# Top-32 attention with a highway layer: one list of 72 maxima in place of 144, folds over two pairs at once

## The chip, the cores and the metric

One core of a Trainium2 chip runs the whole program. The metric is the device time of one execution in microseconds (us); lower is better. Before the change three runs gave 965.99, 966.19 and 967.7 us, median 966.19.

## The reference

```python
# q, k, v: (8 batches, 8 heads, 576 rows, 64), fp32
scores = scale * np.matmul(q, k.transpose(0, 1, 3, 2))          # 576 x 576 for each batch and head
kth = np.partition(scores, -32, axis=-1)[..., -32:-31]          # 32nd largest score of each row
scores = np.where(scores >= kth, scores, -1e9)
attn = softmax(scores);  x = attn @ v                           # back to 4608 x 512
H = np.maximum(x @ w_h, 0.0);  T = sigmoid(x @ w_t + b_t)
out = T * H + (1.0 - T) * x
```

## The kernel before, in words

A *tile* is 128 query rows of one head against all 576 keys. Two tiles make a *pair*; the program numbers 144 pairs, 18 to a batch. Four pairs (two at the end of a batch, where the last 64 rows of two heads share a tile) make a *group*, 40 in all, and a finished group goes through the highway layer.

The instructions are pinned: each engine runs its own in the order in which they are written, so `keep_in_program_order` (L35) is the line that the profile gives for nearly all of them, and tiles are told apart by name. The main loop (L636) is a software pipeline. In step n:

- VectorE (DVE) folds pair n (`tree`, L181): `hi`, the larger of score i and score i+288, read from the scores in PSUM (`ps`) and their copy in SBUF (`z`); then `hh`, the larger of the two halves of `hi`, 144 wide.
- GpSimd (POOL) forms the smaller ones that the folds threw away (`minima`, L194): `hl` (144 wide) and `lo` (288 wide), by integer subtraction and addition, two instructions each.
- DVE runs the lists of pair n-1 (`chain`, L207), the two tiles in turns: MAX8 and MATCH_REPLACE8 on `hh` twice (the best 16 out of 144), MAX8 on the two halves of `hl` and on `lo` (8 each), all gathered in `w2` (168 wide); then `m3`, a replace, and `m4`, whose last entry is the 32nd largest score.
- ScalarE (ACT) makes the penalties `pen` of pair n-2 from `m4` (`mask`), TensorE (PE) transposes `z` plus penalty (`trans`), ACT takes the exponential (`et`), PE multiplies pair n-3 with v (`av`).
- PE computes the scores of pair n+1 into `ps`, which has one buffer: it waits for `hi` of pair n. ACT copies them to `z` (`evac`), and `hi` of pair n+1 waits for that.
- At a group's end DVE forms `rinv`, POOL normalises `x`, and over the next three steps PE transposes x (`xtps`, in a PE queue where later scores stand behind it), the two matrix products follow, DVE forms `d` twice, POOL adds `o`, and a DMA stores it. `settle` puts margins in `room`, `slack` and `reach` on POOL. If a margin is ever violated, an exact second pass runs.

Of the kernel before, what the change touches and what calls it, by code (L numbers as in the profile page):

```python
# [9 lines left out]
ALU = mybir.AluOpType  # L10
AX = mybir.AxisListType
FP32 = mybir.dt.float32
# [5 lines left out]
TINY = 1.0e-20  # L18
WIDE = 600.0
J = 4  # L20
NZ = 6
NPEN = 3


class Pinned:


    def __init__(self, tc, engine):
        self._tc, self._engine = tc, engine
# [33 lines left out]
class Ops:  # L63


    def __init__(self, ctx, tc, shared, exact):
        self.nc = tc.nc if exact else PinnedCore(tc)
        self.__dict__.update(shared)
        self.exact = exact
        s = "g" if exact else ""  # L70

        def pool(name, bufs, **kw):
            return ctx.enter_context(tc.tile_pool(name=name + s, bufs=bufs, **kw))

# [76 lines left out]
    def scores(self, n, g, pi, prep):  # L153
# [13 lines left out]
                    )  # L167
        self.st[n] = dict(ps=ps)

    def evac(self, n):  # L170
        nc, P, S = self.nc, self.P, self.S
        ps = self.st[n]["ps"]
        if self.exact:
            sc = self.scpool.tile([P, 2, S], FP32, tag="sc", name="sc")
            nc.scalar.copy(sc[:], ps[:, :, 0:S])
        else:
            sc = self.zbufs[n % NZ][:, :, 0:S]
            nc.scalar.activation(sc, ps[:, :, 0:S], AF.Relu)
        self.st[n]["sc"] = sc

    def tree(self, n):  # L181
        nc, P, S = self.nc, self.P, self.S
        H1, H2 = S // 2, S // 4
        sc = self.st[n]["sc"]
        hi = self.treepool.tile([P, 2, H1], FP32, tag="hi", name="hi")
        lo = self.treepool.tile([P, 2, H1], FP32, tag="lo", name="lo")
        hh = self.treepool.tile([P, 2, H2], FP32, tag="hh", name="hh")
        hl = self.treepool.tile([P, 2, H2], FP32, tag="hl", name="hl")
        ps = self.st[n].pop("ps")
        nc.vector.tensor_tensor(hi[:], ps[:, :, 0:H1], sc[:, :, H1:S], ALU.max)  # L190
        nc.vector.tensor_tensor(hh[:], hi[:, :, 0:H2], hi[:, :, H2:H1], ALU.max)
        self.st[n]["tree"] = (hi, hh, hl, lo)

    def minima(self, n):  # L194


        H1, H2 = self.S // 2, self.S // 4
        gp, S = self.nc.gpsimd, self.S
        hi, hh, hl, lo = self.st[n]["tree"]
        sci, hii, loi = [a.bitcast(I32) for a in (self.st[n]["sc"], hi[:], lo[:])]  # L200
        hhi, hli = hh[:].bitcast(I32), hl[:].bitcast(I32)
        gp.tensor_tensor(hli, hii[:, :, 0:H2], hhi, ALU.subtract)
        gp.tensor_tensor(hli, hli, hii[:, :, H2:H1], ALU.add)
        gp.tensor_tensor(loi, sci[:, :, 0:H1], hii, ALU.subtract)
        gp.tensor_tensor(loi, loi, sci[:, :, H1:S], ALU.add)

    def chain(self, g, t, hh, hl, lo):  # L207


        nc, P, S = self.nc, self.P, self.S  # L210
        H2, H4 = S // 4, S // 8
        W = H2 + 24
        vec = nc.vector
        m1, m2, m4 = g.m1[:, t, :], g.m2[:, t, :], g.m4[:, t, :]
        w2 = g.w2[:, t, :]
        vec.max(m1, hh)
        yield
        w1 = self.wpool.tile([P, H2], FP32, tag="w1", name="w1")
        vec.match_replace(w1[:], m1, hh, NEG)
        yield  # L220
        vec.max(m2, w1[:])
        yield
        vec.match_replace(w2[:, 0:H2], m2, w1[:], NEG)
        yield
        vec.max(w2[:, H2 : H2 + 8], hl[:, 0:H4])
        yield
        vec.max(w2[:, H2 + 8 : H2 + 16], hl[:, H4:H2])
        yield
        vec.max(w2[:, H2 + 16 : W], lo)
        yield  # L230
        m3 = self.wpool.tile([P, 8], FP32, tag="m3", name="m3")
        vec.max(m3[:], w2)
        yield
        w3 = self.wpool.tile([P, W], FP32, tag="w3", name="w3")
        vec.match_replace(w3[:], m3[:], w2, NEG)
        yield
        vec.max(m4, w3[:])

    def chain_exact(self, g, t, cur):
        nc, P, S = self.nc, self.P, self.S  # L240
# [15 lines left out]
                yield  # L256

    def lists(self, n, g, pi):
        nc, P, S, H = self.nc, self.P, self.S, self.H
        if pi == 0:  # L260
            for name in ("m1", "m4") if self.exact else ("m1", "m2", "m4"):
                setattr(g, name, self.lpool.tile([P, H, 8], FP32, tag=name, name=name))
            if not self.exact:
                g.w2 = self.lpool.tile([P, H, S // 4 + 24], FP32, tag="w2", name="w2")
        t0 = 2 * pi
        if self.exact:
            sc = self.st[n]["sc"]
            gens = [self.chain_exact(g, t0 + i, sc[:, i, :]) for i in range(2)]
        else:
            hi, hh, hl, lo = self.st[n].pop("tree")  # L270
            gens = [
                self.chain(g, t0 + i, hh[:, i, :], hl[:, i, :], lo[:, i, :])
                for i in range(2)
            ]
        return gens
# [25 lines left out]
    def mask(self, n, g, pi, tis=(0, 1)):  # L301
        nc, P, S = self.nc, self.P, self.S
        sc = self.st[n]["sc"]
        z = self.zbufs[n % NZ]
        pen = None if self.exact else self.pens[n % NPEN]
        for ti in tis:
            t = 2 * pi + ti
            if self.exact:
                low = self.wpool.tile([P, S], FP32, tag="wk", name="low")
                nc.vector.tensor_scalar(  # L310
                    low[:], sc[:, ti, :], g.m4[:, t, 7:8], NEG, ALU.is_lt, ALU.mult
                )
                nc.vector.scalar_tensor_tensor(
                    out=z[:, ti, 0:S],
                    in0=sc[:, ti, :],
                    scalar=g.m1[:, t, 0:1],
                    in1=low[:],
                    op0=ALU.subtract,
                    op1=ALU.add,
                )  # L320
            else:
                nc.scalar.activation(
                    pen[:, ti, 0:S],
                    sc[:, ti, :],
                    AF.Relu,
                    bias=g.m4[:, t, 7:8],
                    scale=-1.0,
                )
        self.st[n].update(z=z, pen=pen)
# [158 lines left out]
def kernel(  # L488
# [31 lines left out]
    nc.vector.tensor_scalar_mul(nident[:], ident[:], -STEEP)  # L520
    zbufs = []
    for i in range(NZ):
        zt = const([P, 2, nck * P], FP32, f"z{i}")
        nc.gpsimd.memset(zt[:, :, S : nck * P], NEG)
        zbufs.append(zt)
    pens = []
# [28 lines left out]
    with ExitStack() as cm:  # L555
# [77 lines left out]
        early[0][4]()  # L633
        ffn = []
        step = 0
        while step < NPR + 4 or ffn:  # L636
            n = step
            if n + 1 < NHP:
                for piece in early[n + 1][1:4]:
# [4 lines left out]
                load_weights()  # L644
            if have(n):
                ops.tree(n)
                ops.minima(n)
            if weights and n > 2:
                cast_weights()
            if have(n - 2):  # L650
                ops.mask(n - 2, *pairs[n - 2], tis=(0,))
            post = None
            if ffn:
                pre, post = ffn.pop(0)
                pre()
            if have(n - 3):
                g, pi = pairs[n - 3]
                ops.av(n - 3, g, pi, preps[g.b][2])
            if have(n - 2):
                ops.mask(n - 2, *pairs[n - 2], tis=(1,))  # L660
            if have(n + 1):
                g, pi = pairs[n + 1]
                ops.scores(n + 1, g, pi, preps[g.b])
                ops.evac(n + 1)
            if n + 1 < NHP:
                early[n + 1][4]()
            gens = ops.lists(n - 1, *pairs[n - 1]) if have(n - 1) else []
            ops.run(gens, 4)
            if post:
                post()  # L670
            ended = have(n - 3) and pairs[n - 3][1] == len(pairs[n - 3][0].pairs) - 1
            if ended:
                ops.run(gens, 5)
                ops.norm(pairs[n - 3][0])
            ops.run(gens)
            if have(n - 2):
                ops.trans(n - 2)
            for piece in pieces.pop(n, []):
                piece()
            if have(n - 1):  # L680
                g, pi = pairs[n - 1]
                if pi == len(g.pairs) - 1:
                    ops.settle(g)
            if ended:
                g = pairs[n - 3][0]
                ffn += [
                    (lambda g=g: ops.ffn_x(g), None),
                    (lambda g=g: ops.ffn_h(g), lambda g=g: ops.ffn_d(g)),
# [90 lines left out]
```

## Time and profile before

| | |
|---|---|
| median of three runs | 966.19 us |
| the profiled execution, its span | 965.6 us, 963.7 us |
| DVE busy | 906.9 us (94% of the span) |
| POOL, PE, ACT busy | 763.5, 749.1, 710.6 us |
| mean granted TensorE clock | 0.902 of full speed |

A row of the timeline gives the start, the busy time and the operation; busy times of neighbours on DVE overlap by a little under 0.1 us, so the cost of an instruction in a full queue is the distance from its start to the next one's start.

### The profile page before, as it was taken

The page shows a single profiled execution, that of the slowest core. Times are in us where ns is not written, and L with a number is a line of the kernel's source. Part 1 is how long each engine was busy: PE and PEld are TensorE (multiplying, and loading weights), DVE is VectorE, ACT ScalarE, POOL GpSimd, SP SyncE. Part 2 cuts the span into 40 slices and gives each one's busy share as a digit, 9 for nine tenths or more (in the row PEclk, how much of TensorE's full clock was granted, in tenths as well). Part 3 has the DMA queues.
Part 4 walks back from the last instruction along what each step waited for, and adds up shares of the span by engine and source line. Part 5 has one row for each costly group of instructions (what it writes and reads, how often), then busy time and mean ns, then how long its engine had stood idle before and what let it go on. Part 6 is the DMA issues. An engine that isn't in the chain of part 4 may idle for free.

```text
span 963.7 us, 20478 instructions
## 1 busy us (share of the span) xinstructions
PE 749.1 (78%) x6554; PEld 524.6 (54%) x6601; DVE 906.9 (94%) x4162; ACT 710.6 (74%) x1321; POOL 763.5 (79%) x802
## 2 busy tenths in 40 slices
PE   5757887878887887778877878787887788777874
PEld 3545555655655555556555555555555555545552
DVE  2879999999999999999999999999999999999992
ACT  3748777887777877787776877688777787767762
POOL 6798888788878878888887788878887787888861
PEclk8779998999898999899998999899999899989896
DMA  5622110122101320022101212012200110000000
GB/s 115 180 64 49 48 49 13 43 50 69 29 12 43 72 63 12 17 71 64 49 12 40 53 49 50 12 44 56 67 25 12 44 49 12 12 18 12 13 12 20
DMA packets 123332, 41.52 MB, mean 43 GB/s; under 512 B 117457, under 2 KB 117457, under 8 KB 123217
## 3 DMA queue, kind: packets, MB, share of 16 engines
q1 hardware_dynamic: 122000, 39.84, 16.5%
q8 instruction: 54, 0.88, 0.4%
q14 instruction: 62, 0.50, 0.2%
q10 hardware_dynamic: 1216, 0.30, 0.1%
HBM read 30.67 MB, written 9.44 MB: 42 GB/s over the span
## 4 chain that ended last, share of the span: by engine, by line
DVE 79%; POOL 8%; PE 7%; SPq 2%; ACT 1%; issue 1%; DMA 1%; POOLq 0%; DVEq 0%
DVE w L35 37%; DVE m L35 22%; DVE hi L35 9%; DVE hh L35 6%; DVE d L35 5%; POOL lo L35 3%; PE ps L35 3%; POOL hl L35 2%; PE zt L35 1%; PE xtps L35 1%; POOL x L35 1%; SPq L103 1%; PE zr L35 1%; SPq L100 1%; ACT z L35 1%
## 5 line engine op out<-in xcount | busy, mean ns | idle before, releaser
L35 PE MATMUL ps<-kT,qT 64*128 64x64 f32 (+3 forms) x1280 | 232.4, 491 | 68.3 <-DVE hi L35 67.9
L35 ACT ACTIVATE pen<-z,m 128x576 bf16<-128x576 f32 x288 | 224.4, 780 | 66.0 <-DVE m L35 65.9
L35 DVE MAX8 m<-w 128x8 f32<-128x168 f32 (+1 forms) x864 | 235.6, 318 | 0.0
L35 PE MATMUL zt<-ident,z 128*128 128x128 f32 x1152 | 234.5, 296 | 0.0
L35 PE MATMUL zt<-nident,pen 128*128 128x128 bf16 x1152 | 222.6, 230 | 0.0
L35 POOL TENSOR_TENSOR hl<-hi,hh 128x288 int32<-128x288 int32 x144 | 114.5, 795 | 125.8 <-DVE hh L35 125.8
L35 ACT ACTIVATE z<-ps 128x1152 f32<-128x1152 f32 x144 | 163.1, 1132 | 67.9 <-PE ps L35 65.1
L35 POOL TENSOR_TENSOR lo<-lo,z 128x576 int32<-128x576 int32 x144 | 203.7, 1414 | 11.3
L35 PEld LDWEIGHTS ps<-kT,qT 64*128 64x128 f32 (+1 forms) x1280 | 116.6, 198 | 174.2 <-issue 94.5
L35 POOL TENSOR_TENSOR lo<-z,hi 128x576 int32<-128x576 int32 x144 | 203.4, 1412 | 0.0
L35 PEld LDWEIGHTS zt<-ident,z 128*128 128x128 f32 x1152 | 175.3, 152 | 22.4
L35 ACT ACTIVATE et<-zt 128x512 bf16<-128x512 f32 x288 | 166.9, 600 | 26.0 <-PE zt L35 25.0
L35 DVE MATCH_REPLACE8 w<-m,w 128x144 f32<-128x144 f32 (+1 forms) x576 | 173.5, 313 | 0.0
L35 PEld LDWEIGHTS <-pen 128*128 128x128 bf16 x1440 | 165.3, 115 | 1.8 <-ACT pen L35 1.7
L35 DVE TENSOR_TENSOR hi<-ps,z 128x576 f32<-128x576 f32 x144 | 108.3, 752 | 28.7 <-ACT z L35 28.6
L35 POOL TENSOR_TENSOR hl<-hl,hi 128x288 int32<-128x288 int32 x144 | 114.7, 797 | 11.3
L35 DVE MAX8 w<-lo 128x8 f32<-128x288 f32 x288 | 116.6, 450 | 0.3 <-POOL lo L35 0.3
L35 PEld LDWEIGHTS <-et 128*128 128x128 bf16 (+1 forms) x1600 | 71.7, 104 | 38.1 <-ACT et L35 14.8
L35 DVE MAX8 w<-hl 128x8 f32<-128x72 f32 x576 | 91.5, 226 | 0.0
L35 PE MATMUL zr<-v,et 128*128 128x65 bf16 (+1 forms) x1600 | 85.1, 199 | 6.0 <-ACT et L35 4.1
L35 PE MATMUL xtps<-ident,x 128*128 128x128 f32 (+1 forms) x160 | 29.6, 316 | 74.8 <-POOL x L35 73.3
L35 PE MATMUL zr<-ident,z 128*128 128x128 f32 x288 | 80.1, 331 | 4.8 <-ACT xs L35 4.8
(62 smaller groups left out, 1103.8 us busy)
## 6 DMA issues: line engine op xcount, KB each, us to landing
kin<-in_k_dram SPq DMA_DIRECT2D x64, 128.0 KB, 2.6
vin<-in_v_dram SPq DMA_DIRECT2D x64, 128.0 KB, 2.6
out_dram<-o SPq DMA_DIRECT2D x32, 256.0 KB, 2.2
qin<-in_q_dram SPq DMA_DIRECT2D x62, 128.0 KB, 2.6
kin<-in_k_dram SPq DMA_DIRECT2D x64, 16.0 KB, 2.3
vin<-in_v_dram SPq DMA_DIRECT2D x64, 16.0 KB, 2.3
w<-in_moe_w_h_dram SPq DMA_DIRECT2D x2, 512.0 KB, 4.2
w<-in_moe_w_t_dram SPq DMA_DIRECT2D x2, 512.0 KB, 7.4
```

Of the source, the lines that this page charges most:

```text
L35: return self._tc.keep_in_program_order(fn(*args, **kw))
L100: eng.dma_start(t[:, 0:J, hh, :], src(h, 0, JP).rearrange("(p j) d -> p j d", j=J))
L103: eng.dma_start(t[0:R, J, hh, :], src(h, JP, S))
```

## The change

- Folds from `hh` on run once for two pairs (a *quad*, 4 tiles): `tree` only forms `hi`; in odd steps `folds` forms `hh` (4 x 144), a third level `h3` (4 x 72) and, straight into `w2`, the 72 smaller values of that level.
- The lists start on `h3`: 72 wide in place of 144. `w2` stays 168 wide: what is left of `h3`, the 72 smaller ones, and 24 from `hl` and `lo`.
- `minima` runs once for a quad and overwrites `hh` and `hi` with `hl` and `lo`; a dependency that was added by hand lets it start after the folds.
- The chain is cut in two: `tops` (four tiles in turns) in the even step after the folds, `rest` two tiles in the next odd step and two late ones reaching into the even step behind it. Masks, transposes, `av` and the highway layer come two steps later.
- `z` has three buffers of four tiles in place of six of two.

```diff
-NZ = 6
+NZ = 3
 def tree(self, n):
+        if n % 2 == 0:
+            self.quads[k] = tuple(
+                self.treepool.tile([P, 4, w], FP32, tag=name, name=name, bufs=bufs)
+                for name, w, bufs in (("hi", H1, 3), ("hh", H2, 3), ("h3", H3, 2))
+            )
-        nc.vector.tensor_tensor(hi[:], ps[:, :, 0:H1], sc[:, :, H1:S], ALU.max)
-        nc.vector.tensor_tensor(hh[:], hi[:, :, 0:H2], hi[:, :, H2:H1], ALU.max)
+        nc.vector.tensor_tensor(
+            hi[:, half, :], ps[:, :, 0:H1], self.st[n]["sc"][:, :, H1:S], ALU.max
+        )
+    def folds(self, k, g, pi):
+        vec.tensor_tensor(hh[:], hi[:, :, 0:H2], hi[:, :, H2:H1], ALU.max)
+        a, b = hh[:, :, 0:H3], hh[:, :, H3:H2]
+        vec.tensor_tensor(h3[:], a, b, ALU.max)
+        return vec.tensor_tensor(
+            g.w2[:, 2 * pi : 2 * pi + 4, H3:H2], a, b, ALU.min
+        )
 def minima(self, k, after):
-        gp.tensor_tensor(hli, hii[:, :, 0:H2], hhi, ALU.subtract)
-        gp.tensor_tensor(hli, hli, hii[:, :, H2:H1], ALU.add)
-        gp.tensor_tensor(loi, sci[:, :, 0:H1], hii, ALU.subtract)
-        gp.tensor_tensor(loi, loi, sci[:, :, H1:S], ALU.add)
+        head = gp.tensor_tensor(hhi, hii[:, :, 0:H2], hhi, ALU.subtract)
+        self.tc.add_manual_dep(
+            head.ins,
+            after.ins.name,
...
+        )
+        gp.tensor_tensor(hhi, hhi, hii[:, :, H2:H1], ALU.add)
+        gp.tensor_tensor(hii, sci[:, :, 0:H1], hii, ALU.subtract)
+        gp.tensor_tensor(hii, hii, sci[:, :, H1:S], ALU.add)
-    def chain(self, g, t, hh, hl, lo):
+    def tops(self, g, t, h3, hl):
-        vec.max(m1, hh)
+        vec.max(m1, h3)
...
+    def rest(self, g, t, lo):
         vec.max(w2[:, H2 + 16 : W], lo)
...
 main loop
-            if have(n - 2):
-                ops.mask(n - 2, *pairs[n - 2], tis=(0,))
+            if have(n - 4):
+                ops.mask(n - 4, *pairs[n - 4], tis=(0,))
...
-            gens = ops.lists(n - 1, *pairs[n - 1]) if have(n - 1) else []
-            ops.run(gens, 4)
-            if post:
-                post()
...
+            if n % 2:
+                gens = ops.lists_rest(n // 2 - 1, *pairs[n - 3]) if have(n - 3) else []
+                late = gens[2:]
+                gens = gens[0:2]
+                ops.run(gens)
+                if post:
+                    post()
+                ops.run(late, 2)
+            else:
+                ops.run(late)
+                gens = ops.lists(n - 2, *pairs[n - 2]) if have(n - 2) else []
+                ops.run(gens, 2)
+                if post:
+                    post()
+                if ended:
+                    ops.norm(pairs[n - 5][0])
+                ops.run(gens)
```

On DVE, a step of the steady part before (`w` with a number is `w1`, `w2` or `w3`, `m` is `m1` to `m4`; sizes are those of the output):

```order
L35 TENSOR_TENSOR hi<-ps,z_69 128x576
L35 TENSOR_TENSOR hh<-hi 128x288
L35 MAX m_8820<-hh 128x8 x2
L35 MATCH_REPLACE w_8918<-m_8820,hh 128x144
L35 MATCH_REPLACE w_8920<-m_8820,hh 128x144
L35 MAX m_8821<-w_8918 128x8
L35 MAX m_8821<-w_8920 128x8
L35 MATCH_REPLACE w_8823<-m_8821,w_8918 128x144
L35 MATCH_REPLACE w_8823<-m_8821,w_8920 128x144
L35 MAX w_8823<-hl 128x8 x4
L35 MAX w_8823<-lo 128x8 x2
L35 MAX m_8932<-w_8823 128x8
```

The whole list of one pair stands behind the folds of the next pair. Now an odd step on DVE, from its `hi` to the `hi` of the even step (`h` is `h3`; `hi` as the input of a MAX is what was `lo`):

```order
L35 TENSOR_TENSOR hi<-ps,z_69 128x576
L35 TENSOR_TENSOR hh<-hi 128x576
L35 TENSOR_TENSOR h_8600<-hh 128x288
L35 TENSOR_TENSOR w_8691<-hh 128x4x72
L35 MAX w_8313<-hi 128x8 x2
L35 MAX m_8730<-w_8313 128x8
L35 MAX m_8732<-w_8313 128x8
L35 MATCH_REPLACE w_8734<-m_8730,w_8313 128x168
L35 MATCH_REPLACE w_8736<-m_8732,w_8313 128x168
L35 MAX m_8437<-w_8734 128x8
L35 MAX m_8437<-w_8736 128x8
L35 MAX w_8313<-hi 128x8 x2
```

The three folds now stand in a row behind the second `hi` of a quad, and the list work between them and the next `hi` belongs to the quad before.

On POOL, before, around the end of a group (a store's `o` and a normalised `x` next to each other, as at one place in a batch):

```order
L35 TENSOR_TENSOR hl<-hi,hh 128x288
L35 TENSOR_TENSOR hl<-hl,hi 128x288
L35 TENSOR_TENSOR lo<-z_65,hi 128x576
L35 TENSOR_TENSOR lo<-lo,z_65 128x576
L35 TENSOR_TENSOR o<-x,d 64x512
L35 TENSOR_TENSOR x<-xs,rinv 128x512
```

Two short ones follow the four of one pair. And now, the two kinds of quad that take turns (one with `room`, one with `o` and `x`):

```order
L35 TENSOR_TENSOR hi<-z_67,hi 128x1152
L35 TENSOR_TENSOR hi<-hi,z_67 128x1152
L35 TENSOR_TENSOR room<-m_9414,w_9284 128x24
L35 TENSOR_TENSOR slack<-m_9413,m_9414 128x8
L35 COPY reach<-m_9412 128x8
L35 TENSOR_TENSOR hh<-hi,hh 128x576
L35 TENSOR_TENSOR hh<-hh,hi 128x576
L35 TENSOR_TENSOR hi<-z_69,hi 128x1152
L35 TENSOR_TENSOR hi<-hi,z_69 128x1152
L35 TENSOR_TENSOR o<-x,d 128x512
L35 TENSOR_TENSOR x<-xs,rinv 128x512
```

The four instructions of a pair became four of twice the size for a quad, and `o` and `x` now stand together behind them in four of a batch's nine quads.

## Rows read from the trace of the kernel before

**Rows 1.** The page, the chain that ended last: shares of the span by engine.
```profile
DVE 79%; POOL 8%; PE 7%; SPq 2%; ACT 1%; issue 1%; DMA 1%; POOLq 0%; DVEq 0%
```

**Rows 2.** One window: length; busy us of PE, PEld, DVE, ACT, POOL; PEclk; DMA.
```profile
79.00:938.00 859.00, 687.06 (x6123) 482.78 (x6167) 849.54 (x3916) 658.43 (x1222) 696.50 (x729) 0.92 0.15 38
```

**Rows 3.** Timeline of DVE, one step: start, busy time, operation, count.
```profile
482.50 0.74 DVE L35 TENSOR_TENSOR hi<-ps,z 128x576 f32<-128x576 f32 x1
483.28 0.46 DVE L35 TENSOR_TENSOR hh<-hi 128x288 f32<-128x288 f32 x1
483.65 0.51 DVE L35 MAX8 m<-hh 128x8 f32<-128x144 f32 x2
484.08 0.08 DVE L35 MATCH_VALUE_LOAD w<-m,hh 128x8 f32 x1
...
484.62 0.52 DVE L35 MAX8 m<-w 128x8 f32<-128x144 f32 x2
...
485.60 0.64 DVE L35 MAX8 w<-hl 128x8 f32<-128x72 f32 x4
486.14 0.81 DVE L35 MAX8 w<-lo 128x8 f32<-128x288 f32 x2
...
487.33 0.08 DVE L35 MATCH_VALUE_LOAD w<-m,w 128x8 f32 x1
...
488.40 0.75 DVE L35 TENSOR_TENSOR hi<-ps,z 128x576 f32<-128x576 f32 x1
```

**Rows 4.** Chain of waits, 470 to 500 us (start, us, what): `d`, `rinv`.
```profile
473.20 0.60 DVE d L35
...
494.53 0.10 DVE rinv L35
```

**Rows 5.** Timeline of DVE: first steps, and the longest wait after them.
```profile
40.39 0.75 DVE L35 TENSOR_TENSOR hi<-ps,z 128x576 f32<-128x576 f32 x1
...
72.07 0.76 DVE L35 TENSOR_TENSOR hi<-ps,z 128x576 f32<-128x576 f32 x1 [6.60 <-ACT z L35]
```

**Rows 6.** Timeline of POOL: three of a pair's minima and an `o`.
```profile
472.21 0.80 POOL L35 TENSOR_TENSOR hl<-hl,hi 128x288 int32<-128x288 int32 x1
472.97 1.41 POOL L35 TENSOR_TENSOR lo<-z,hi 128x576 int32<-128x576 int32 x1
474.46 1.41 POOL L35 TENSOR_TENSOR lo<-lo,z 128x576 int32<-128x576 int32 x1
475.83 1.27 POOL L35 TENSOR_TENSOR o<-x,d 128x512 f32<-128x512 f32 x1
```

**Rows 7.** Timelines of DVE and POOL: `hh` under a POOL instruction, two cases.
```profile
179.64 1.05 DVE L35 TENSOR_TENSOR hh<-hi 128x288 f32<-128x288 f32 x1
...
179.33 1.04 POOL L35 TENSOR_TENSOR x<-xs,rinv 128x512 f32<-128x512 f32 x1
...
40.30 2.78 POOL L35 TENSOR_SCALAR wh<-w 128x1024 bf16<-128x1024 f32 x1
...
41.17 0.48 DVE L35 TENSOR_TENSOR hh<-hi 128x288 f32<-128x288 f32 x1
```

**Rows 8.** Timelines of POOL, PE and ACT: from `x` to `z`, two cases.
```profile
482.31 1.04 POOL L35 TENSOR_TENSOR x<-xs,rinv 128x512 f32<-128x512 f32 x1
...
486.10 1.13 ACT L35 ACTIVATE z<-ps 128x1152 f32<-128x1152 f32 x1
...
292.58 1.03 POOL L35 TENSOR_TENSOR x<-xs,rinv 128x512 f32<-128x512 f32 x1
...
293.67 1.11 PE L35 MATMUL xtps<-ident,x 128*128 128x128 f32 x4 [3.89 <-POOL x L35]
...
297.71 1.13 ACT L35 ACTIVATE z<-ps 128x1152 f32<-128x1152 f32 x1 [0.94 <-PE ps L35]
```

**Rows 9.** Waits in the steady stretch, 79 to 938 us: total, times, longest.
```profile
ACT pen L35 <- DVE m L35: 64.6, 52, 2.1
...
PE xtps L35 <- POOL x L35: 63.4, 30, 4.2
```

More of the change, by code (lines that the diff above doesn't have):

```diff
@@ L66, in __init__ @@
     def __init__(self, ctx, tc, shared, exact):
+        self.tc = tc
         self.nc = tc.nc if exact else PinnedCore(tc)
@@ L89, in __init__ @@
         self.st = {}
+        self.quads = {}
     def load_pair(self, src, hp, name, eng=None):
@@ L168, in scores, with zview @@
         self.st[n] = dict(ps=ps)
+    def zview(self, n):
+        return self.zbufs[n // 2 % NZ][:, 2 * (n % 2) : 2 * (n % 2) + 2, :]
     def evac(self, n):
@@ L176, in evac @@
         else:
-            sc = self.zbufs[n % NZ][:, :, 0:S]
+            sc = self.zview(n)[:, :, 0:S]
             nc.scalar.activation(sc, ps[:, :, 0:S], AF.Relu)
@@ L182, in tree @@
         nc, P, S = self.nc, self.P, self.S
[L183 to L188, printed above, removed]
-        ps = self.st[n].pop("ps")
-        nc.vector.tensor_tensor(hi[:], ps[:, :, 0:H1], sc[:, :, H1:S], ALU.max)
@@ L191, in tree @@
-        nc.vector.tensor_tensor(hh[:], hi[:, :, 0:H2], hi[:, :, H2:H1], ALU.max)
-        self.st[n]["tree"] = (hi, hh, hl, lo)
-    def minima(self, n):
+        H1, H2, H3 = S // 2, S // 4, S // 8
+        k, half = n // 2, slice(2 * (n % 2), 2 * (n % 2) + 2)
+        if n % 2 == 0:
[3 more added lines that the diff above has]
+            )
@@ new lines, in tree @@
+        hi = self.quads[k][0]
+        ps = self.st[n].pop("ps")
+        nc.vector.tensor_tensor(
+            hi[:, half, :], ps[:, :, 0:H1], self.st[n]["sc"][:, :, H1:S], ALU.max
+        )
+    def folds(self, k, g, pi):
+        vec, P, S, H = self.nc.vector, self.P, self.S, self.H
+        H1, H2, H3 = S // 2, S // 4, S // 8
+        if pi == 0:
+            g.w2 = self.lpool.tile([P, H, H2 + 24], FP32, tag="w2", name="w2")
+        hi, hh, h3 = self.quads[k]
+        vec.tensor_tensor(hh[:], hi[:, :, 0:H2], hi[:, :, H2:H1], ALU.max)
[4 more added lines that the diff above has]
+        )
@@ L197, in minima @@
+    def minima(self, k, after):
         H1, H2 = self.S // 2, self.S // 4
         gp, S = self.nc.gpsimd, self.S
-        hi, hh, hl, lo = self.st[n]["tree"]
-        sci, hii, loi = [a.bitcast(I32) for a in (self.st[n]["sc"], hi[:], lo[:])]
-        hhi, hli = hh[:].bitcast(I32), hl[:].bitcast(I32)
-        gp.tensor_tensor(hli, hii[:, :, 0:H2], hhi, ALU.subtract)
-        gp.tensor_tensor(hli, hli, hii[:, :, H2:H1], ALU.add)
-        gp.tensor_tensor(loi, sci[:, :, 0:H1], hii, ALU.subtract)
@@ L205, in minima @@
-        gp.tensor_tensor(loi, loi, sci[:, :, H1:S], ALU.add)
-    def chain(self, g, t, hh, hl, lo):
+        hi, hh, h3 = self.quads[k]
+        z = self.zbufs[k % NZ]
+        sci, hii, hhi = [a[:].bitcast(I32) for a in (z, hi, hh)]
+        head = gp.tensor_tensor(hhi, hii[:, :, 0:H2], hhi, ALU.subtract)
+        self.tc.add_manual_dep(
+            head.ins,
+            after.ins.name,
+            mybir.DependencyInfo(
+                mybir.DependencyClass.Sync, mybir.DependencyReason.DATA
+            ),
+            reason="after the folds",
+        )
@@ L210, in chain @@
+        gp.tensor_tensor(hhi, hhi, hii[:, :, H2:H1], ALU.add)
+        gp.tensor_tensor(hii, sci[:, :, 0:H1], hii, ALU.subtract)
+        gp.tensor_tensor(hii, hii, sci[:, :, H1:S], ALU.add)
+    def tops(self, g, t, h3, hl):
         nc, P, S = self.nc, self.P, self.S
-        H2, H4 = S // 4, S // 8
-        W = H2 + 24
+        H2, H3 = S // 4, S // 8
         vec = nc.vector
-        m1, m2, m4 = g.m1[:, t, :], g.m2[:, t, :], g.m4[:, t, :]
-        w2 = g.w2[:, t, :]
-        vec.max(m1, hh)
+        m1, m2, w2 = g.m1[:, t, :], g.m2[:, t, :], g.w2[:, t, :]
+        vec.max(m1, h3)
@@ L217, in chain @@
         yield
-        w1 = self.wpool.tile([P, H2], FP32, tag="w1", name="w1")
-        vec.match_replace(w1[:], m1, hh, NEG)
+        w1 = self.wpool.tile([P, H3], FP32, tag="w1", name="w1")
+        vec.match_replace(w1[:], m1, h3, NEG)
         yield
@@ L222, in chain @@
         yield
-        vec.match_replace(w2[:, 0:H2], m2, w1[:], NEG)
+        vec.match_replace(w2[:, 0:H3], m2, w1[:], NEG)
         yield
-        vec.max(w2[:, H2 : H2 + 8], hl[:, 0:H4])
+        vec.max(w2[:, H2 : H2 + 8], hl[:, 0:H3])
         yield
-        vec.max(w2[:, H2 + 8 : H2 + 16], hl[:, H4:H2])
-        yield
+        vec.max(w2[:, H2 + 8 : H2 + 16], hl[:, H3:H2])
+    def rest(self, g, t, lo):
+        nc, P, S = self.nc, self.P, self.S
+        H2 = S // 4
+        W = H2 + 24
+        vec = nc.vector
+        w2 = g.w2[:, t, :]
         vec.max(w2[:, H2 + 16 : W], lo)
@@ L236, in chain @@
         yield
-        vec.max(m4, w3[:])
+        vec.max(g.m4[:, t, :], w3[:])
     def chain_exact(self, g, t, cur):
@@ L258, in lists @@
     def lists(self, n, g, pi):
-        nc, P, S, H = self.nc, self.P, self.S, self.H
+        P, H = self.P, self.H
         if pi == 0:
@@ L262, in lists @@
                 setattr(g, name, self.lpool.tile([P, H, 8], FP32, tag=name, name=name))
-            if not self.exact:
-                g.w2 = self.lpool.tile([P, H, S // 4 + 24], FP32, tag="w2", name="w2")
         t0 = 2 * pi
@@ L267, in lists, with lists_rest @@
             sc = self.st[n]["sc"]
[L268 to L275, printed above, removed]
+            return [self.chain_exact(g, t0 + i, sc[:, i, :]) for i in range(2)]
+        hi, hh, h3 = self.quads[n // 2]
+        return [
+            self.tops(g, t0 + i, h3[:, i, :], hh[:, i, :]) for i in range(4)
+        ]
+    def lists_rest(self, k, g, pi):
+        hi = self.quads.pop(k)[0]
+        return [self.rest(g, 2 * pi + i, hi[:, i, :]) for i in range(4)]
     @staticmethod
@@ L303, in mask @@
         sc = self.st[n]["sc"]
-        z = self.zbufs[n % NZ]
+        z = self.zview(n)
         pen = None if self.exact else self.pens[n % NPEN]
@@ L522 @@
     for i in range(NZ):
-        zt = const([P, 2, nck * P], FP32, f"z{i}")
+        zt = const([P, 4, nck * P], FP32, f"z{i}")
         nc.gpsimd.memset(zt[:, :, S : nck * P], NEG)
@@ L635 @@
         step = 0
-        while step < NPR + 4 or ffn:
+        late = []
+        while step < NPR + 6 or ffn:
             n = step
@@ L646 @@
                 ops.tree(n)
-                ops.minima(n)
+                if n % 2:
+                    ops.minima(n // 2, ops.folds(n // 2, *pairs[n - 1]))
             if weights and n > 2:
                 cast_weights()
-            if have(n - 2):
-                ops.mask(n - 2, *pairs[n - 2], tis=(0,))
+            if have(n - 4):
+                ops.mask(n - 4, *pairs[n - 4], tis=(0,))
             post = None
@@ L655 @@
                 pre()
[L656 to L660, printed above, removed]
+            if have(n - 5):
+                g, pi = pairs[n - 5]
+                ops.av(n - 5, g, pi, preps[g.b][2])
+            if have(n - 4):
+                ops.mask(n - 4, *pairs[n - 4], tis=(1,))
             if have(n + 1):
@@ L666 @@
                 early[n + 1][4]()
-            gens = ops.lists(n - 1, *pairs[n - 1]) if have(n - 1) else []
-            ops.run(gens, 4)
-            if post:
-                post()
[L671 to L677, printed above, removed]
+            ended = have(n - 5) and pairs[n - 5][1] == len(pairs[n - 5][0].pairs) - 1
+            if n % 2:
+                gens = ops.lists_rest(n // 2 - 1, *pairs[n - 3]) if have(n - 3) else []
[14 more added lines that the diff above has]
+                ops.run(gens)
+            if have(n - 4):
+                ops.trans(n - 4)
             for piece in pieces.pop(n, []):
                 piece()
-            if have(n - 1):
-                g, pi = pairs[n - 1]
+            if n % 2 == 0 and have(n - 3):
+                g, pi = pairs[n - 3]
                 if pi == len(g.pairs) - 1:
@@ L684 @@
             if ended:
-                g = pairs[n - 3][0]
+                g = pairs[n - 5][0]
                 ffn += [
```

## The prediction

> **What bounds the kernel now.** The chain that ended last comes first: 79% of it is DVE [rows 1]. The windows then say where: from 79 to 938 us DVE is busy 849.5 of 859 us, the others 658 to 697 [rows 2]. So in that stretch the time is the number of DVE instructions times their spacing, and what other engines wait for costs nothing until DVE waits too. The timeline of one step gives the spacings [rows 3]: `hi` to `hi` is 488.40 - 482.50 = 5.90 us, without a gap. Outside the stretch, DVE waits for the first loads until 40.39, once 6.60 us at 72.07 [rows 5], and a chain of other engines follows its last list. The profiled execution took 965.6 us, 0.6 below the median of 966.19; I work from the former and add 0.6.
>
> **The change part by part, on DVE.** All from rows 3, for two pairs (a quad):
>
> - Before: 2 x 5.90 = 11.80. Of a step, `hi` takes 0.78 to `hh`, `hh` 0.37 to the first MAX, the first four rounds of both tiles 485.60 - 483.65 = 1.95, four MAX of 72 from `hl` 0.54, the rest 488.40 - 486.14 = 2.26.
> - The rest and the `hl` maxima are only moved: 2 x (2.26 + 0.54) = 5.60 stays.
> - The first rounds shrink from 144 to 72. A MAX of 144 takes (484.08 - 483.65)/2 = 0.215, one of 72 takes 0.54/4 = 0.135, the size that is needed. A MATCH_REPLACE of 144 with its load takes (484.62 - 484.08)/2 = 0.27; at 72 the trace has none. Bounds: 0.27 if it doesn't shrink, 0.135 if it were as quick as a MAX. I take 0.27 - 0.08 = 0.19, the step that the MAX shows. Four tiles: 8 x 0.135 + 8 x 0.19 = 2.60 instead of 3.90.
> - The folds. One `hi` is followed by `hh`, which needs it: 0.78. The other is followed by work that doesn't: by the law of `hh` (0.37 for 288; a MAX shows 0.08 for 72 more) 0.37 + 4 x 0.08 = 0.69, bounds 0.6 and 0.78. `hh` of 576 with `h3` behind it that needs it: as `hi`, 0.78, bounds 0.69 and 0.9. `h3` and the minimum, 288 each: 0.37 each, bounds 0.37 and 0.46 (the busy time). Sum 2.99 instead of 2.30.
>
> A quad is 5.60 + 2.60 + 2.99 = 11.19, against 11.80: 0.61 less, 72 times 44 us. The bounds together: replaces that don't shrink cost 8 x 0.08 = 0.64 more and the folds at their upper ends 0.39 more, so a quad could lose 0.42 (30 us slower); at the lower ends it would win 8 x 0.055 + 0.18 = 0.62 on top (89 us faster). The sizes asked for of MAX (72) and of the folds (288 and 576) stand in the rows, only the replace's doesn't, so I stay near the middle.
>
> **What the deeper pipeline gives back.** DVE is gapless only from the `hi` of pair 4, at 40.39 [rows 5]. By then the kernel before has done four folds and three lists, 4 x 1.15 + 3 x 4.75 = 18.9. After, the folds of two quads (6.0), one quad's tops (2.60 + 1.08) and of its rest 2.26 + 1.19 (`lo` to the load at 487.33 [rows 3]) fit there: 13.1. DVE's remaining work falls from 144 x 5.90 - 18.9 = 830.7 to 72 x 11.19 - 13.1 = 792.6, by 38. That is the gain if nothing new waits. The tail behind the last `m4` has the same steps in the same order as before; I count nothing, bounds -2 and +2. The loads hang on step numbers that stay, the stores come two steps later behind the same queue; nothing. A buffer of `z` is now filled again one step after its last transposes instead of three, but the scores that fill it stand behind those transposes in PE's queue anyway; nothing.
>
> **POOL and the folds.** The folds read two operands from SBUF, and rows 7 show what that means: an `hh` that starts at 179.64 while POOL has an `x` running (179.33 to 180.37) takes 1.05 in place of 0.46; it ends 0.32 after the `x`. So a fold waits until POOL's instruction is over. `hi` and `d` read PSUM and aren't held. The added dependency keeps a quad's own minima away, but not what is left of the quad before. I lay one quad out from the start of its `hh` (0): the minimum ends at 0.78 + 0.37 + 0.46 = 1.61, POOL starts. A POOL instruction of 576 takes 1.41, 0.08 to a dependent one; 288 takes 0.80, so each 288 costs 0.61 and 1152 takes 2.63, which no row shows (bounds 2 x 1.41 = 2.82 and 2.4) [rows 6]. Minima: 1.49 + 1.49 + 2.71 + 2.63 = 8.3, ending at 9.9. In four quads of nine, `o` (1.27) [rows 6] and `x` (1.04) [rows 7] follow: 12.24. DVE is back at the next `hh` after 11.19 + 0.60 (`d`) + 0.10 (`rinv`) [rows 4] = 11.89. The fold is held for 12.24 - 0.14 - 11.89 = 0.2. In the other five quads POOL is done by about 10.7.
>
> The same `x` then holds PE: `xtps` stands ahead of the next scores. From the end of `x` to the end of `z` the trace has two lengths: (486.10 + 1.13) - (482.31 + 1.04) = 3.9, and, after PE had stood idle 3.89 and ran slower, (297.71 + 1.13) - (292.58 + 1.03) = 5.2 [rows 8]. After the change `z` is there at 16.1 or 17.5, and the even `hi` is due at 11.89 + 0.2 + 0.78 + 0.74 + 2.26 + 1.19 = 17.1. So nothing, or 0.4. Which of the two it is hangs on how long PE stands idle first; before, its waits for `x` were 63.4/30 = 2.1 on average [rows 9], well below the 3.89 of the slow case, so I take half: 0.2. Together 0.4 in each of 32 quads: 13 us. Bounds: 0, and 1.2 (both mishaps and a late `d`), 38 us. The kernel before has the `hh` wait seven times at 0.55, 4 us, which go. The masks, for which ACT waited 64.6 us [rows 9], now have half a step to spare; ACT was not in DVE's way, so nothing.
>
> The 6.60 us wait at 72.07 comes while POOL casts weights and `x` is late. Those casts now stand behind longer minima, and folds are held there too; I take it as unchanged, bounds 7 less and 8 more. One cast shows something: `hh` at 41.17 lies under the cast of `wh` (40.30 to 43.08) and takes 0.48, so a cast doesn't hold it [rows 7]. The Trainium skill says otherwise (SBUF — State Buffer, section "SBUF: two separate sides"): a VectorE instruction with two SBUF inputs and any GpSimd instruction that reads SBUF lock each other out, the first one keeping the ports to its end. By that rule the folds of quad 2, which come while two casts of 2.78 follow the minima of quad 1, would wait for one or for both, some 2 to 4 us, and the sum would be about 940; by the row it is nothing, and I go by the row.
>
> **Sum.** 965.6 - 38 + 13 - 4 = 936.6; with 0.6 for the median, 937, which I predict.
>
> **Rivals.**
>
> 1. *Nothing waits.* POOL's long instructions take 2.4 and `x` comes in time; the wait at 72 us goes too. 966 - 38 - 4 - 7 = 917. For it: the layout misses by 0.2 only, within the error of 2.63. Against: at the one place in a batch where `o` and `x` stood together before, PE waited 3.89 for `x` [rows 8].
> 2. *The late `x` sets every group's end.* PE stands idle before each `xtps`, the products behind it run slower, `z` and then `d` come late: 1.2 in each of 32 quads, and 8 more early on: 966 - 38 - 4 + 38 = 962, with the 8 of the early part 970. For it: the case at 293 us, where exactly this order stood on POOL [rows 8]. Against: there `z` took 5.2 from `x`, and the layout leaves 4.8, so the loss is the difference and no more.
> 3. *Slower: POOL holds the folds.* Each POOL instruction of 1152 would take 3.3 rather than 2.63 (four tiles strided, output over input). The minima then end at 11.3, `x` at 13.6, and the fold waits 13.6 - 0.14 - 11.89 = 1.55 in 32 quads: 50 us, with the 8 of the early part 58, against a gain of 38 + 4 = 42: 982. It decides from 42/32 = 1.3 us for each of these quads, which is 3.2 for an instruction of 1152. Against: sizes 288 and 576 give a line with a small fixed part, and `lo` written over itself takes the same 1.41 as `lo` from `z` and `hi` [rows 6].
> 4. *The margin fails* and the exact pass runs: several times the time. The list of 72 must hold 16 values above the threshold; 32 largest scores fall on about 72 x (1 - (71/72)^32) = 26 different places out of 72, so 15 or fewer is out of reach. Under 1%, left out of the range.
>
> **How the numbers follow.** Forecast (928 to 946) 0.47, rival 1 (912 to 927) 0.22, rival 2 (947 to 963) 0.22, rival 3, with the upper bounds of the DVE costs, 0.09. The range of 8 in 10 leaves out rival 3, the last of rival 2 and the first of rival 1: 914 to 960; the forecast's own is 928 to 946. Less than 0.2% (2 us) is about what a measurement of this kernel can't tell from no change; that sliver around 966 lies between rivals 2 and 3 and gets 0.04. Slower by more than that 0.06, faster by more 0.90.
>
> **What would show it.** Right: a quad takes about 11.2 us on DVE without `d`, a MATCH_REPLACE of 72 follows its neighbour by 0.19, the POOL instruction of 1152 takes 2.6, `hh` is longer by about 0.2 in four quads of nine, and DVE is 97 to 98% busy. Wrong: replaces that don't shrink; `h3` or the minimum at 1 us or more, which would mean POOL still at work there; `hi` waiting for `z` every few steps, at over 1 us; or POOL instructions over 3 us.

## The result, and the profile after

The changed kernel takes 932.35 us (median of 4 runs, 931.12 to 933.4), the one before in the same session 966.89 (965.99 to 967.7): a ratio of 0.9642, interval 0.9623 to 0.9662. The forecast was 937 with a range of 914 to 960. The profiled execution took 933.4 us, its span is 931.6; before they were 965.6 and 963.7, so 32.1 us of span are to be accounted for.

The page's chain that ended last, and the window that answers to [rows 2], of the changed kernel:

```profile
DVE 74%; POOL 12%; PE 7%; ACT 3%; issue 2%; SPq 1%; DMA 0%; POOLq 0%; ACTq 0%; DVEq 0%
```

```profile
79.00:900.00 821.00, 667.17 (x6159) 468.78 (x6158) 808.12 (x3965) 646.29 (x1221) 657.84 (x456) 0.95 0.16 39
```

DVE is busy 808.12 of 821 us, 98.4%: it still sets the time. POOL's share of the chain has grown from 8% [rows 1] to 12%.

DVE's timeline of one quad (two pairs) of the changed kernel answers to the step in [rows 3]:

```profile
489.24 0.73 DVE L35 TENSOR_TENSOR hi<-ps,z 128x576 f32<-128x576 f32 x1
490.00 0.76 DVE L35 TENSOR_TENSOR hh<-hi 128x576 f32<-128x576 f32 x1
490.80 0.46 DVE L35 TENSOR_TENSOR h<-hh 128x288 f32<-128x288 f32 x1
491.17 0.45 DVE L35 TENSOR_TENSOR w<-hh 128x288 f32<-128x288 f32 x1
491.54 0.81 DVE L35 MAX8 w<-hi 128x8 f32<-128x288 f32 x2
...
493.81 0.67 DVE L35 SCALAR_TENSOR_TENSOR d<-tps,d 128x512 f32<-128x512 f32 x1
...
495.60 0.74 DVE L35 TENSOR_TENSOR hi<-ps,z 128x576 f32<-128x576 f32 x1
496.26 0.08 DVE L35 MATCH_VALUE_LOAD w<-m,w 128x8 f32 x1
...
497.88 0.07 DVE L35 MATCH_VALUE_LOAD w<-m,h 128x8 f32 x1
...
498.68 0.63 DVE L35 MAX8 m<-w 128x8 f32<-128x72 f32 x4
...
501.12 0.73 DVE L35 TENSOR_TENSOR hi<-ps,z 128x576 f32<-128x576 f32 x1
```

From `hi` to the `hi` after next it is 501.12 - 489.24 = 11.88; without the `d` (0.60, [rows 4]) 11.28, where 11.19 was forecast and two steps before took 11.80. The folds run behind one another without a hold: `hi` 0.76, `hh` 0.80, `h3` 0.37, the minimum 0.37, the other `hi` 0.66: 2.96 (forecast 2.99). Four replaces of 72 with their loads take 498.68 - 497.88 = 0.80, so 0.20 each (forecast 0.19).

The other engines' part: a `hh` that waits, with what POOL did meanwhile (timelines of DVE and POOL), and the two waits of the steady stretch that answer to [rows 9] (the first line from 79 to 900 us, the second from 79 to 905: total, times, longest).

```profile
319.02 0.94 DVE L35 TENSOR_TENSOR hh<-hi 128x576 f32<-128x576 f32 x1
...
314.47 2.65 POOL L35 TENSOR_TENSOR hi<-hi,z 128x1152 int32<-128x1152 int32 x1
317.08 1.26 POOL L35 TENSOR_TENSOR o<-x,d 128x512 f32<-128x512 f32 x1
318.31 1.03 POOL L35 TENSOR_TENSOR x<-xs,rinv 128x512 f32<-128x512 f32 x1
```

```profile
DVE hi L35 <- ACT z L35: 6.4, 6, 3.1
...
PE xtps L35 <- POOL x L35: 51.0, 29, 2.8
```

POOL's minimum of 1152 takes 2.65 (forecast 2.63). `o` and `x` follow, `x` ends at 319.34, and the `hh` takes 0.18 more than the 0.76 above. DVE waits for `z` six times, and one of these, 3.1 us, lies at 82 us, at the end of the head (the first 85 us, in which POOL casts the weights).

### The profile page after: what moved, and what is told of

Its sections match the earlier page's. It is cut to its first block, busy times and chain, and to the rows that moved or that the text cites. A ratio compares the mean times of both kernels' runs of the same rounds, so it can differ in the third digit from the quotient of the medians.

```text
span 931.6 us, 20391 instructions
## 1 busy us (share of the span) xinstructions
PE 730.9 (78%) x6601; PEld 511.4 (55%) x6601; DVE 878.4 (94%) x4234; ACT 699.7 (75%) x1321; POOL 722.1 (78%) x511
## 4 chain that ended last, share of the span: by engine, by line
DVE 74%; POOL 12%; PE 7%; ACT 3%; issue 2%; SPq 1%; DMA 0%; POOLq 0%; ACTq 0%; DVEq 0%
DVE w L35 35%; DVE m L35 17%; DVE hi L35 8%; POOL hi L35 6%; DVE hh L35 5%; DVE d L35 4%; POOL hh L35 3%; DVE h L35 3%; PE ps L35 2%; PE zt L35 2%; POOL o L35 1%; PE zr L35 1%; PE xtps L35 1%; POOL x L35 1%; SPq L102 1%
## 5 line engine op out<-in xcount | busy, mean ns | idle before, releaser
L35 PE MATMUL ps<-kT,qT 64*128 64x64 f32 (+3 forms) x1280 | 222.3, 473 | 51.4 <-DVE hi L35 50.5
L35 POOL TENSOR_TENSOR hh<-hi,hh 128x576 int32<-128x576 int32 x72 | 101.7, 1412 | 167.3 <-DVE w L35 167.1
L35 PE MATMUL zt<-ident,z 128*128 128x128 f32 x1152 | 225.4, 289 | 0.0
L35 DVE MAX8 m<-w 128x8 f32<-128x168 f32 (+1 forms) x864 | 203.9, 284 | 0.0
L35 POOL TENSOR_TENSOR hi<-hi,z 128x1152 int32<-128x1152 int32 x72 | 191.2, 2656 | 5.6
L35 POOL TENSOR_TENSOR hi<-z,hi 128x1152 int32<-128x1152 int32 x72 | 189.4, 2631 | 5.6
L35 ACT ACTIVATE et<-zt 128x512 bf16<-128x512 f32 x288 | 161.8, 601 | 15.9 <-PE zt L35 14.5
L35 DVE MATCH_REPLACE8 w<-m,w 128x72 f32<-128x72 f32 (+1 forms) x576 | 148.6, 267 | 0.0
L35 DVE MAX8 w<-hi 128x8 f32<-128x288 f32 x288 | 116.5, 445 | 0.0
L35 POOL TENSOR_TENSOR hh<-hh,hi 128x576 int32<-128x576 int32 x72 | 101.6, 1411 | 5.6
L35 DVE MAX8 w<-hh 128x8 f32<-128x72 f32 x576 | 84.1, 218 | 0.0
```

What stands on the lines that cost most here:

```text
L35: return self._tc.keep_in_program_order(fn(*args, **kw))
```

## The experiments

The times before were 966.43 in the session of the first four runs and 966.29 in that of the last four. Every ratio is to these.

**The third level taken out.** All else of the change stays: folds over two pairs, the chain in two parts, one stage more.

```diff
-        vec.tensor_tensor(h3[:], a, b, ALU.max)
-        return vec.tensor_tensor(g.w2[:, 2*pi : 2*pi+4, H3:H2], a, b, ALU.min)
+        return vec.tensor_tensor(hh[:], hi[:, :, 0:H2], hi[:, :, H2:H1], ALU.max)
...
-            self.tops(g, t0 + i, h3[:, i, :], hh[:, i, :]) for i in range(4)
+            self.tops(g, t0 + i, hh[:, i, :], hl[:, i, :]) for i in range(4)
```

> The changed kernel without its third level: folds and minima over two pairs, the chain in two parts, the later masks all stay, but the lists start on hh, 144 wide, and hl has a tile of its own. Theory (the gain is DVE time saved by the list of 72, less the longer folds): a quad costs DVE 5.60 for what is the same, 3.90 for the first rounds (rows of before) and 0.76 + 0.66 + 0.69 = 2.11 for the folds, 11.6 us where the changed kernel has 11.28; 953 to 958 us in all. Rival (the gain comes from larger instructions and from masks that no longer wait on DVE's last result): as the changed kernel, 930 to 936.

Measured: 947.95 us (945.94 to 949.76), ratio 0.981 (0.9794 to 0.9827). That is the theory's side, though 5 below its figures. DVE's timeline of a quad there:

```profile
482.55 0.73 DVE L35 TENSOR_TENSOR hi<-ps,z 128x576 f32<-128x576 f32 x1
...
491.13 0.68 DVE L35 SCALAR_TENSOR_TENSOR d<-hps,xh 128x512 f32<-128x512 f32 x1
491.73 0.18 DVE L35 RECIPROCAL rinv<-xs 64x8 f32<-64x8 f32 x1
...
494.84 0.73 DVE L35 TENSOR_TENSOR hi<-ps,z 128x576 f32<-128x576 f32 x1
```

From `hi` to the `hi` after next 12.29; less `d` (491.73 - 491.13 = 0.60) and `rinv` (0.10, [rows 4]) it is 11.59: the step is as expected. What the expectation left out is that the waits of the kernel before went too: from 79 to 900 us `hh` takes 0.758 on average, never held, and no `d` waits. Of the 34 us between before and after, the third level brings 947.95 - 932.35 = 15.6, the quad and the split the other 18.5. On DVE alone the third level is worth 11.59 - 11.28 = 0.31 a quad, 22 us; so some 6 are taken back by the medians, and 10 between the two profiled executions (945.94 and 933.4). It is taken back by waits: `hh` is held again (3.8 us in all, below), `d` waits 1.9, and `z` 2.4 more.

**The third level alone,** on the kernel before, pair by pair, with the minima likewise started after the folds.

```diff
+        h3 = self.treepool.tile([P, 2, H3], FP32, tag="h3", name="h3")
+        a, b = hh[:, :, 0:H3], hh[:, :, H3:H2]
+        nc.vector.tensor_tensor(h3[:], a, b, ALU.max)
+        self.after = nc.vector.tensor_tensor(
+            g.w2[:, 2 * pi : 2 * pi + 2, H3:H2], a, b, ALU.min
+        )
```

> The kernel before with the third level alone: pair by pair, lists on h3 of 72, minima held until the folds are done, chain in one piece, masks where they were. Theory (72 wide lists pay only if the two added folds run for two pairs at once): a step costs 0.78 + 0.47 + 0.22 + 0.22 = 1.69 for the folds and 1.34 + 0.54 + 2.26 for the lists, 5.83 us against 5.90 before; less than 10 us gained, and x comes 0.5 later, so 955 to 964. Rival (the shorter list is the whole gain, quads don't matter): 930 to 938.

Measured: 999.23 us (998.96 to 1006.31), ratio 1.0333 (1.0315 to 1.035): slower than before, and neither theory had that. The profiled execution took 1004.98, so in the trace 39 us are to be accounted for. Its timelines of DVE and POOL, then its groups and its wait for `z` (79 to 975 us):

```profile
501.35 0.74 DVE L35 TENSOR_TENSOR hi<-ps,z 128x576 f32<-128x576 f32 x1
502.13 0.98 DVE L35 TENSOR_TENSOR hh<-hi 128x288 f32<-128x288 f32 x1
...
508.14 0.76 DVE L35 TENSOR_TENSOR hi<-ps,z 128x576 f32<-128x576 f32 x1 [0.32 <-ACT z L35]
...
501.76 1.04 POOL L35 TENSOR_TENSOR x<-xs,rinv 128x512 f32<-128x512 f32 x1
```

```profile
L35 DVE TENSOR_TENSOR hh<-hi 128x288 f32<-128x288 f32 x135 | 82.7, 613 | 4.6
...
L35 DVE TENSOR_TENSOR h<-hh 128x144 f32<-128x144 f32 x135 | 46.6, 345 | 4.7
```

```profile
DVE hi L35 <- ACT z L35: 16.2, 27, 1.7
```

The step is nearly as cheap as expected: 508.14 - 501.35 = 6.79, less the 0.32 wait, the hold of `hh` (0.98 - 0.46 = 0.52) and the 0.08 by which neighbours overlap where none waits, is 5.87; 5.83 was expected, and 5.90 was the step before [rows 3]. But `hh` takes 0.613 on average where 0.46 is unheld: 135 x 0.153 = 20.7 us, against 135 x 0.027 = 3.6 before. Waits for `z` are 16.2 (before 2.5), for `d` 5.9 (before 2.1). `h` is held as well: 0.345 where 0.31 is unheld, 135 x 0.035 = 5 us. That is 17 + 14 + 4 + 5 = 40 us, about the whole loss. The minima of a pair start later, behind `h3`, and with `o` or `x` behind them they run into the next `hh` one step of 5.9 later. From the start of an `hh`, POOL needs 1.1 (the folds), 4.5 (the four minima) and 1.04 (`x`), 6.6, and the next `hh` comes after 5.9. So the folds over two pairs do more than cut instructions: they meet POOL half as often, and the 12.2 of the forecast's layout compares with 11.9.

**The minima not held.** `hl` and `lo` get tiles of their own, and the added dependency goes. `hi` and `hh` have two buffers there in place of three; from 79 to 900 us DVE waits only for `z` (4.6 us) and `d` (0.5), so the missing buffers cost it nothing.

```diff
-        head = gp.tensor_tensor(hhi, hii[:, :, 0:H2], hhi, ALU.subtract)
-        self.tc.add_manual_dep(
-            head.ins,
-            after.ins.name,
...
+        gp.tensor_tensor(hli, hii[:, :, 0:H2], hhi, ALU.subtract)
```

> The changed kernel with hl and lo in tiles of their own and without the added dependency, so that POOL may start as soon as hh is there, beside h3 and the minimum. Theory (a fold that reads two operands from SBUF waits until POOL's instruction is over): h3 starts first, the minimum finds the 1.41 us POOL instruction running and takes up to 1.8 us instead of 0.45; about 1.3 more per quad, 1000 to 1030 us. Rival (POOL and the folds run beside each other, the dependency protects nothing but the data in place): 925 to 932, POOL being done 0.7 earlier.

Measured: 1004.25 us (1003.92 to 1005.33), ratio 1.0385 (1.0368 to 1.0403): the theory. Its group of the minimum (79 to 900 us), and a case on DVE and POOL:

```profile
L35 DVE TENSOR_TENSOR w<-hh 128x288 f32<-128x288 f32 x62 | 103.3, 1666 | 0.0
```

```profile
485.62 0.46 DVE L35 TENSOR_TENSOR h<-hh 128x288 f32<-128x288 f32 x1
485.99 1.66 DVE L35 TENSOR_TENSOR w<-hh 128x288 f32<-128x288 f32 x1
...
485.66 1.68 POOL L35 TENSOR_TENSOR hl<-hi,hh 128x576 int32<-128x576 int32 x1 [2.98 <-DVE hh L35]
```

The minimum takes 1.67 in place of 0.45, each time from 79 us on (62 to 900 us, 67 in all): 67 x 1.21 = 81 us. Some 7 us of waits go (`hh` is never held here, `z` and `d` wait less), which leaves 74 where 1004.25 - 932.35 = 72 were measured. POOL's instruction is lengthened as well, 1.68 against 1.41 (1.67 or more in 69 of 72): each holds the other.

**The chain not split a step apart.** The rest of two tiles stands behind the tops of its own quad, the other two behind the next folds.

```diff
                 ops.run(gens)
+                gens = ops.lists_rest(n // 2 - 1, *pairs[n - 2]) if have(n - 2) else []
+                late = gens[2:]
+                ops.run(gens[0:2])
```

> The changed kernel with the chain's two parts no longer a stage apart: the rest of two tiles directly behind the tops in the even step, that of the other two behind the folds in the next odd step. Theory (the distance is there because a quad's minima take POOL 8.3 us from the end of the folds): lo is wanted 8.2 us after hh starts and is there at 10.0, so DVE waits 1.7 in every quad; a quad takes about 13.0 instead of 11.3, less what d hides: 1020 to 1055 us. Rival (DVE is the only bound, where the parts stand doesn't matter): 930 to 936.

Measured: 1007.93 us (1006.06 to 1008.91), ratio 1.0418 (1.04 to 1.0436): the theory's direction, 12 below its range. DVE's waits there, 79 to 900 us:

```profile
DVE w L35 <- POOL hi L35: 31.2, 46, 1.1
DVE d L35 <- PE hps L35: 15.6, 16, 1.8
DVE hi L35 <- ACT z L35: 11.6, 19, 0.8
DVE d L35 <- ACT tps L35: 7.8, 6, 1.3
DVE rinv L35 <- ACT xs L35: 5.1, 16, 0.8
```

Together 71.3 us, against 8.3 after. The lists wait for the minima of their own quad, as expected, but by 0.68 on average and not in every quad; more than half of the sum is waits for PE and ACT. One quad, on DVE, shows how they belong together:

```profile
343.92 0.76 DVE L35 TENSOR_TENSOR hh<-hi 128x576 f32<-128x576 f32 x1
...
353.97 0.82 DVE L35 MAX8 w<-hi 128x8 f32<-128x288 f32 x2 [1.12 <-POOL hi L35]
...
357.03 0.76 DVE L35 TENSOR_TENSOR hh<-hi 128x576 f32<-128x576 f32 x1
```

From `hh` to its own quad's `lo` it is 10.05, and from there to the next `hh` 3.06: 13.11. In the trace 55 of the 66 quads from 90 us on take 13.1, with or without `rinv`, and whether or not DVE waited for `d` or `z` before: what it waits there it waits less for `lo`. The mean is 13.27, after the change 12.14, and 66 x 1.13 = 75 us is the difference measured. The stage apart is what hides POOL's 8.3 us. The other eleven take 13.9 to 14.5, 11 us more in all; `d` is late in each, and why is not traced.

**The same kernel again,** beside the next three.

> The changed kernel itself, for the three beside it: 931 to 934 us by every theory.

Measured: 933.05 us (931.24 to 934.05), ratio 0.9653 (0.964 to 0.9666).

**The store and its `o` two steps later,** behind the next quad's minima.

```diff
-                        lambda g=g: (ops.ffn_e(g), ops.ffn_o(g, out_rows(g))),
+                        lambda g=g: (ops.ffn_e(g), stores.append((step, g))),
...
+            if stores and n >= stores[0][0] + 2:
+                g = stores.pop(0)[1]
+                ops.ffn_o(g, out_rows(g))
```

> The changed kernel with each group's o (and its store) two steps later, behind the next quad's minima, so that x stands directly behind the minima. Theory (x behind o holds hh in 24 quads by 0.16 and makes z and d late): x comes 1.25 earlier, the holds (3.9 us) and part of the late z and d (5.2 us in the steady stretch) go: 924 to 929. Rival (what is left beside DVE's own time doesn't come from x): 931 to 934.

Measured: 924.34 us (924.25 to 925.37), ratio 0.9565 (0.9552 to 0.9579): 8.7 less than the same session's 933.05. Its waits, 79 to 900 us:

```profile
DVE hi L35 <- ACT z L35: 3.4, 1, 3.4
...
PE xtps L35 <- POOL x L35: 17.8, 17, 2.9
```

With `o` out of the way `x` comes earlier: PE waits 17.8 us for it instead of 51.0, and DVE for `z` only in the head. No `d` is late; `hh` is down from 0.815 to 0.790 on average. What the late `x` cost is thereby measured: 9 us with all that hangs on it, of which these waits and holds make up 6.6.

**The weight casts on ACT** instead of POOL.

```diff
-            ops.nc.gpsimd.tensor_scalar_mul(dst, w32[:], by)
+            ops.nc.scalar.mul(dst, w32[:], by)
```

> The changed kernel with the five casts of the weights on ACT instead of POOL. Theory (in the first 85 us POOL is late because of the casts, folds wait for its long instructions and z for x: 1.1 + 0.7 + 2.3 + 0.4 + 3.1 us): 924 to 927. Rival (that stretch is set by loads, by PE or by ACT, which now has 5 us more to do): 931 to 936.

Measured: 924.35 us (923.54 to 926.08), ratio 0.9567 (0.9554 to 0.958), again 8.7 less. The head on DVE's timeline, first after the change (with POOL's part), then with the casts moved:

```profile
57.83 1.88 DVE L35 TENSOR_TENSOR hh<-hi 128x576 f32<-128x576 f32 x1
59.74 1.18 DVE L35 TENSOR_TENSOR h<-hh 128x288 f32<-128x288 f32 x1
60.84 0.45 DVE L35 TENSOR_TENSOR w<-hh 128x288 f32<-128x288 f32 x1
...
71.82 2.77 DVE L35 TENSOR_TENSOR h<-hh 128x288 f32<-128x288 f32 x1
74.50 0.86 DVE L35 TENSOR_TENSOR w<-hh 128x288 f32<-128x288 f32 x1
81.92 0.76 DVE L35 TENSOR_TENSOR hi<-ps,z 128x576 f32<-128x576 f32 x1 [3.09 <-ACT z L35]
...
59.06 6.01 POOL L35 TENSOR_SCALAR wt<-w 128x1024 bf16<-128x1024 f32 x2
...
71.24 3.02 POOL L35 TENSOR_TENSOR hi<-hi,z 128x1152 int32<-128x1152 int32 x1
74.24 1.69 POOL L35 TENSOR_SCALAR bt<-bt 128x512 bf16<-128x512 f32 x1
```

```profile
57.81 0.76 DVE L35 TENSOR_TENSOR hh<-hi 128x576 f32<-128x576 f32 x1
...
74.17 0.73 DVE L35 TENSOR_TENSOR hi<-ps,z 128x576 f32<-128x576 f32 x1
```

The same `hi` stands at 81.92 after the change and at 74.17 here: 7.75 us of the 8.7 are won by then. They are the holds of four folds (1.12 + 0.72 + 2.31 + 0.41 = 4.56; the first under the end of a minimum, 56.45 to 59.09) and the 3.09 wait, 7.65.

**Both.** The last two edits together.

> Both edits, the later o and the casts on ACT. If both reasons hold the gains add up, since they lie in different stretches: 916 to 922. If one of them is wrong: that of the other alone, 924 to 929.

Measured: 916.82 us (915.97 to 917.12), ratio 0.9481 (0.9468 to 0.9494). It is the fastest of all: 16.2 below 933.05, where the two gains add to 17.4. They are nearly independent, one in the steady stretch and one in the head.

## Why the prediction was right

Each step of the sum, measured in the profiled executions:

- **The quad.** Forecast 11.19, measured 11.28, against 11.80. The folds came out 0.03 cheaper (2.96); the replaces of 72 at 0.20 instead of 0.19 make 8 x 0.01 = 0.08 more, and the rest is within the rounding of the rows. DVE's work after 40 us thus falls by 830.7 - (72 x 11.28 - 13.1) = 31.6 us, not 38. This term was too good by 6. With every wait, hold, `d` and `rinv` included, a quad takes 12.14 on average from the `hh` at 88.82 to that at 890.00; before, two steps took 12.67 (91.86 to 928.10).
- **`hh` held.** Forecast 32 quads x 0.2 = 6.4. Measured: 23 of the 72 `hh` in the trace last 0.91 to 0.95, longer by 0.16, 3.8 us in all (a 24th, at 57.83, belongs to the head); that the kernel before loses about as much this way (4 us, [rows 7]) was right too. The layout had four such quads in nine and the trace has three: in the fourth `d` falls twice into the quad, and DVE comes later.
- **`z` late.** Forecast 6.4. Measured: 6.4 - 3.1 = 3.3, in five places; `d` waits 1.9 in three, about the 2.1 of before. This and the held `hh` stood at 13 together and were 7.1; the kernel before lost 3.9 to `hh` and 2.5 to `z`. So these waits all but cancel between the two kernels, where +13 - 4 = +9 was counted. This term was too dear by 8: two errors, 6 and 8, that nearly offset each other in the sum. That the sum came within 5 us is to that extent luck; the mechanism is the one that was forecast.
- **The head.** Forecast unchanged. 7.65 us against 6.60 for `z` [rows 5] and 0.9 of holds: unchanged. But its makeup is another: more than half of it is now held folds.
- **The deeper pipeline.** The 5.8 us of work that no longer fits in ahead of pair 4 stood inside the 38, and the trace has on DVE, up to 40.26, just the work that was counted there. The last `m4` ends at 905.8 instead of 938.7, 32.9 sooner; the `hi` of pair 4 started at 40.26 instead of 40.39. Of the 32.9 the terms above give 31; the last 2 are not traced to a place.
- **The tail.** Forecast 0, measured 25.8 against 25.0.

Of the rivals, the first (nothing waits, 917) didn't occur. With `o` and the casts out of the way the kernel takes 916.82, but that the figures meet is no proof of its price: 38 of its sum was DVE's work, which fell by 31.6. The second fell, since `z` was late in five places and not in 32. The third fell at its own figure, 2.65 for an instruction of 1152 where 3.2 was the point of decision. The kernel with free minima shows that its mechanism is real all the same: there the folds do meet POOL, and the kernel is slower than before.

On casts and folds the row was read too broadly. `hh` at 41.17 under a cast took 0.48 [rows 7], and after the change `w` at 60.84 under the cast of `wt` takes 0.45; but `h` at 59.74, which starts 0.68 after that cast does, takes 1.18. The Trainium skill's rule (SBUF — State Buffer, section "SBUF: two separate sides") would have each of them wait to the end of the cast. The trace bears out neither the rule in full nor "a cast doesn't hold it".

## What to carry to other kernels

Where one engine is busy 98% of the time, its instructions counted at their spacing gave the change's size here to within some 20% (38 against 31.6); the waits must then be counted on both sides of the change, since here the ones that went were as large as the ones that came. A cut in VectorE's work can lose if it moves its two-input SBUF operations against GpSimd's: the same third level won 16 us here with folds over two pairs and lost 33 alone. The time after the change named the next steps: what stands between GpSimd's long instructions and a fold (`o`, the casts) was worth 16 us more with no arithmetic changed.

## What the runs showed of the hardware that was not expected

- The hold between a fold and a POOL instruction works both ways. A POOL operation of 576 that started 0.04 into a fold took 1.68 rather than 1.41 (the kernel with free minima). A `room` of 12 elements that began while a `hh` was held took 0.74, where the shortest of its kind took 0.22; the two small ones behind it took 0.52 and 0.41, under the next two folds. The cast at 74.24 took 1.69, the same one before 1.49.

```profile
367.16 0.92 DVE L35 TENSOR_TENSOR hh<-hi 128x576 f32<-128x576 f32 x1
...
366.42 1.05 POOL L35 TENSOR_TENSOR x<-xs,rinv 128x512 f32<-128x512 f32 x1
367.42 0.74 POOL L35 TENSOR_TENSOR room<-m,w 128x12 f32<-128x12 f32 x1
368.12 0.52 POOL L35 TENSOR_TENSOR slack<-m,m 128x4 f32<-128x4 f32 x1
368.58 0.41 POOL L35 COPY reach<-m 128x4 f32<-128x4 f32 x1
```

- A cast (TENSOR_SCALAR) holds a fold that begins shortly after its start (0.68 after: 1.18 in place of 0.46; 0.26 after, under a cast of 512: 0.86 in place of 0.45), and not one that begins 0.87 after it [rows 7] or 1.78 after (60.84). Why it stops holding isn't known.
- TensorE's mean granted clock rose from 0.902 to 0.942 in the profiled executions (0.874 to 0.916 over the other ones before, 0.924 to 0.946 after), though its work is the same; the kernel without the chain's split had 0.900 and the one with the third level alone 0.896. No run here tells why.
